# A Fourier mixer feeding a mixture of experts: expert rounds sized by the mean number of full blocks, from the first batch on, with the end of the last round under a condition

## The chip, the core and the metric

The kernel runs on one core of a Trainium2 chip. The core's engines work side by side, each through its own list of instructions: TensorE (PE, with PEld for its weight loads), VectorE (DVE), ScalarE (ACT), GpSimd (POOL) and SyncE (SP), which here only issues transfers. The metric is the device time of one execution in microseconds (us). Three executions of the kernel before took 744.09, 748.9 and 751.19 us, median 748.9.

## The reference

Two layers follow one another. The first filters each of 8 batches (2,496 rows of 256 numbers) along the rows in the frequency domain. The second sends each of the 19,968 filtered rows to one of 8 experts, the one with the highest score, and multiplies what the expert gives by the softmax weight of that score.

```python
X = np.fft.rfft(x, axis=1)
F = (filt_r + 1j * filt_i)[None, :, :]
y = np.fft.irfft(X * F, n=x.shape[1], axis=1)

logits = x @ w_gate + modality_bias[modality_id]
e_idx = np.argmax(logits, axis=1)
for e in range(E):
    mask = e_idx == e
    h = np.maximum(x[mask] @ w1[e], 0.0)
    out[mask] = gate_w[mask, None] * (h @ w2[e])
```

w1 is 256x1024 and w2 1024x256 for each expert. The inputs are drawn with a fixed seed. Counted in the reference, the experts get these rows after each batch (cumulative; experts 1, 2, 4, 5, 6 and 7 get none):

| after batch | 0 | 1 | 2 | 3 | 4 | 5 | 6 | 7 |
|---|---|---|---|---|---|---|---|---|
| expert 0 | 1258 | 2477 | 3744 | 4989 | 6227 | 7520 | 8767 | 9972 |
| expert 3 | 1238 | 2515 | 3744 | 4995 | 6253 | 7456 | 8705 | 9996 |

The kernel is not told this; its code is the same for any routing.

## The kernel before

**The transform.** A batch goes through three stages of small matrix products (`stage1`, `stage2`, `stage3`), each for a piece of the batch at a time. Between the stages the data go to DRAM and come back in another order: `b1_d` between the first two (stored at L238, loaded by `load_t2`, L433), `b2_d` between the last two (stored at L473, loaded by `load_t4`, L440). Both loads put their tiles into one pool, `bp` (L112), with three buffers under one tag. All of these stores and loads are issued by SP, in order.

**Routing.** `stage3` also computes the scores. `count` and `place` find each row's expert and its place, and `scatter` (L581, an indirect transfer issued by POOL) writes the row into that expert's bin in DRAM, `bins_d`. A batch has 20 scatters.

**Blocks and rounds.** Experts work on blocks of 256 rows of one bin. After a batch is placed, `table` (L599) computes, on DVE, which expert and which block each of the K next turns takes. K is a number that is fixed when the program is built, since the list of instructions is: the round sizes `KR` (L81). Before, a round is as long as the number of blocks that are full whatever the routing (`sure`): 0, 11, 10, 10, 9, 10, 10 after batches 0 to 6. The last round has 25 turns, enough for any routing (85 in all). A turn for which there is no block reads a bin of padding, whose rows are dropped at the output (`bounds_check` at L718).

**One turn.** `load` reads the number of the block and issues the load of its rows (`xs`, L659, on SP). `turn` copies the expert's w1 (L675, DVE) and transposes the rows (L685). Four steps follow, in each of which `up` (L696) makes a quarter of the hidden layer, ACT applies the relu (L701), and `down` (L709) takes a quarter of the turn before. After a turn's last step DVE multiplies by the weight (L716), and POOL scatters the 2x128 rows to `out` (L719).

**The order of work.** The main loop (L823) counts slots, `n`. In a slot stand one piece of each stage of each batch that is due, batches being 14 slots apart, up to a few scatters, and 2.25 expert steps (`STEPS`), if a turn is ready. A turn is not begun before 4 slots after its load (`LAG`). The weights w1 and w2 are loaded in slots 13 to 48. Batch g is placed in slot 45+14g, and its round is opened when its scatters are issued, 10 slots later. Up to slot 60 (`FRONT`, `alone`) the transform also uses PSUM tiles of the experts' pools (`front`, L219). The loop ends at slot 151, and the turns that are left follow alone (L861), the tail. A scheduler may move an instruction of one engine past others within what its dependences allow; it keeps the shape of this order.

Of the kernel before, what the change touches and what calls it, by code (L numbers as in the profile page):

```python
# [13 lines left out]
I32 = mybir.dt.int32  # L14
# [9 lines left out]
def cdiv(a, b):  # L24
    return (a + b - 1) // b
# [3 lines left out]
def kernel(  # L29
# [12 lines left out]
    nc = tc.nc  # L42

    B, S, D = x.shape
    NF = S // 2 + 1
    N = B * S
    E = moe_w_gate.shape[1]
# [22 lines left out]
    BLK = 256  # L70
# [4 lines left out]
    NBLK = cdiv(N, BLK) + E - 1  # L75
    DW = D // 2
    RW = DW + 2


    sure = [max(0, ((g + 1) * S - E * (BLK - 1)) // BLK) for g in range(B)]  # L80
    KR = [0, sure[1]] + [sure[g] - sure[g - 1] for g in range(2, B - 1)]  # L81
    KR.append(NBLK - sum(KR))

    b1_d = nc.dram_tensor("b1_d", (B, NTT, KA, D), BF16, kind="Internal").ap()
    b2_d = nc.dram_tensor("b2_d", (B, NS, KB, D), BF16, kind="Internal").ap()
# [2 lines left out]
    const_pool = ctx.enter_context(tc.tile_pool(name="const", bufs=1))  # L88
# [20 lines left out]
    SCH = 8  # L109
    xp = ctx.enter_context(tc.tile_pool(name="fx", bufs=3))  # L110
    rp = ctx.enter_context(tc.tile_pool(name="fr", bufs=2))
    bp = ctx.enter_context(tc.tile_pool(name="fbig", bufs=3))  # L112
    yp = ctx.enter_context(tc.tile_pool(name="fy", bufs=2))


    marks = {"ld": [], "up": [], "w1": [], "out": [], "pe": []}
# [64 lines left out]
    def ts(out, in_, s1, s2, op0=ALU.mult, op1=ALU.add):  # L181
        nc.vector.tensor_scalar(out, in_, scalar1=s1, scalar2=s2, op0=op0, op1=op1)
# [58 lines left out]
    def input_piece(g, k):  # L241

        stage1(g, k)
        if (k + 1) * EV in [t1 for t0, t1 in TCH]:
            load_x()
# [124 lines left out]
    ts(ecap, eio, float(CAP), -1.0)  # L370
    KMAX = max(KR)
    jio_i = const_pool.tile([P, KMAX], I32)
# [57 lines left out]
    def load_t2(g, c):  # L430
        src = b1_d[g].rearrange("t (jr s) c -> (t jr) s c", jr=4)
        t2 = bp.tile([KB, SCH, D], BF16, tag="t24", name="t2")
        nc.sync.dma_start(t2, src[:, c * SCH:(c + 1) * SCH, :])  # L433
        st[g]["t2", c] = t2
# [142 lines left out]
    def scatter(g, t):  # L577

        rows = P if t < NYF else KA
        with behind("out", 1):  # L580
            ins = nc.gpsimd.indirect_dma_start(  # L581
                out=bins_d[:, :], out_offset=IOA(ap=st[g]["pos"][:rows, t:t + 1], axis=0),
                in_=st[g]["yw"][:rows, t, :], in_offset=None)

        free_of(ins, "bins")
        free_of(ins, "bin_reads")
        tc.add_to_no_dep_group("bins", ins.ins)
        paced(ins)
# [10 lines left out]
    def table(K, last):  # L599

        b2 = [P, K, E]
        ni = tp_.tile([P, E], I32, tag="ni")
        av = tp_.tile([P, E], F32, tag="av")
        if last:
            ts(av, cnt, 1.0, float(BLK - 1))
            nc.vector.tensor_copy(ni, av)
        else:
            nc.vector.tensor_copy(ni, cnt)
        nc.vector.tensor_single_scalar(ni, ni, int(math.log2(BLK)), op=ALU.arith_shift_right)
        nc.vector.tensor_copy(av, ni)  # L610
        nc.vector.tensor_sub(av, av, done)
        incl = tp_.tile([P, E], F32, tag="incl")
        nc.vector.tensor_tensor_scan(incl, ones_sq[:, 0:E], av, 0.0, op0=ALU.mult, op1=ALU.add)
        excl = tp_.tile([P, E], F32, tag="excl")
        nc.vector.tensor_sub(excl, incl, av)
        v = tp_.tile([P, E], F32, tag="v")
        nc.vector.tensor_sub(v, done, excl)
        m = tp_.tile(b2, F32, tag="m")
        jb = jio[:, 0:K, None].to_broadcast(b2)
        nc.vector.tensor_tensor(m, incl[:, None, :].to_broadcast(b2), jb, op=ALU.is_le)  # L620
        ej = tp_.tile([P, K], F32, tag="ej")
        nc.vector.reduce_sum(ej, m, axis=AX.X)
        ec = tp_.tile([P, K], F32, tag="ec")
        nc.vector.tensor_scalar_min(ec, ej, float(E - 1))
        ej_i = tp_.tile([P, K], I32, tag="eji", bufs=3)
        nc.vector.tensor_copy(ej_i, ec)
        nc.vector.tensor_tensor(m, eio[:, None, :].to_broadcast(b2), ej[:, :, None].to_broadcast(b2),
                                op=ALU.is_equal)
        tmp = tp_.tile(b2, F32, tag="mt")
        nc.vector.tensor_mul(tmp, m, v[:, None, :].to_broadcast(b2))  # L630
        lb = tp_.tile([P, K], F32, tag="lb")
        nc.vector.reduce_sum(lb, tmp, axis=AX.X)
        nc.vector.tensor_add(lb, lb, jio[:, 0:K])
        bj = tp_.tile([P, K], F32, tag="bj")
        nc.vector.scalar_tensor_tensor(bj, in0=ej, scalar=float(BPE), in1=lb, op0=ALU.mult, op1=ALU.add)
        nc.vector.tensor_scalar_min(bj, bj, float(E * BPE))
        bj_i = tp_.tile([P, K], I32, tag="bji", bufs=3)
        nc.vector.tensor_copy(bj_i, bj)
        if not last:
            ts(excl, excl, -1.0, float(K))  # L640
            nc.vector.tensor_scalar_max(excl, excl, 0.0)
            nc.vector.tensor_tensor(excl, excl, av, op=ALU.min)
            nc.vector.tensor_add(done, done, excl)
        return ej_i, bj_i

    binv = bins_d.rearrange("(n p i) d -> n p i d", p=P, i=NI)

    def behind(what, n):

        m = marks[what]  # L650
        return tc.issue_after(m[-n]) if len(m) >= n else nullcontext()

    def load(tab, j, last):

        ej_i, bj_i = tab
        with behind("ld", 2):
            bj = nc.values_load(bj_i[0:1, j:j + 1], engines=(ET.SP,), min_val=0, max_val=E * BPE)
        xs = ep.tile([P, NI, RW], I32, tag="xs", bufs=5)
        ld = nc.sync.dma_start(xs, binv[ds(bj, 1)].rearrange("o p i d -> p (o i) d"))  # L659
        tc.add_to_no_dep_group("bin_reads", ld.ins)  # L660
        marks["ld"].append(ld.ins)
        return dict(xs=xs, ej_i=ej_i[0:1, j:j + 1], last=last)
# [63 lines left out]
    def pad_bins():  # L726

        end = tp_.tile([P, E], F32, tag="end")
        nc.vector.tensor_add(end, cnt, ecap)
        end_i = tp_.tile([P, E], I32, tag="endi")  # L730
        ts(end_i, end, 1.0, 1.0)
        for e in range(E):
            r = nc.values_load(end_i[0:1, e:e + 1], engines=(ET.SP,), min_val=0, max_val=E * CAP - BLK)
            ins = nc.sync.dma_start(bins_d[ds(r, BLK)].rearrange("(p i) w -> p i w", i=NI), pad)
            free_of(ins, "bins")
            free_of(ins, "bin_reads")
            tc.add_to_no_dep_group("bins", ins.ins)
# [57 lines left out]
    moe = Experts()  # L795
    tabs = {}
# [4 lines left out]
    def pace(left):  # L801

        if to_bins and left:
            g, t = to_bins[0]
            if t < NY:
                scatter(g, t)
                to_bins[0][1] += 1
                left -= 1
            else:
                if g == B - 1:  # L810
                    pad_bins()
                moe.open(tabs[g], KR[g], g == B - 1)
                to_bins.pop(0)
        return left

# [7 lines left out]
    while True:  # L823
        for g in range(1, B):
            if 0 <= n - g * GAP < NP:
                input_piece(g, n - g * GAP)
        for g in range(B):
            k = n - g * GAP - OFF2
            if (k + LEAD) % 4 == 0 and 0 <= k + LEAD < NS // EV:
                load_t2(g, (k + LEAD) // 4)  # L830
            if 0 <= k <= NS // EV:
                stage2(g, k)
        for g in range(B):
            k = n - g * GAP - OFF3
            if (k + LEAD) % 3 == 0 and 0 <= k + LEAD < NPY:
                load_t4(g, (k + LEAD) // 3)
            if 0 <= k <= NPY + 1:
                stage3(g, k)
            if k == NPY + 2:
                count(g)  # L840
            if k == NPY + 3:
                place(g)
                tabs[g] = table(KR[g], g == B - 1) if KR[g] else None
                to_bins.append([g, 0])
        alone[0] = n < FRONT
        left = 2 if n < (B - 1) * GAP + OFF3 + NPY + 3 else NY
        left = pace(pace(left) if n < FRONT + 10 else left)
        if n >= WSTART and n % 3:
            load_w()
        owed += STEPS  # L850
        while owed >= 1:
            owed -= 1
            outs = len(marks["out"])
            moe.step()
            if len(marks["out"]) == outs:
                left = pace(left)
        n += 1
        if not to_bins and n > (B - 1) * GAP + OFF3 + NPY + 4:
            break
    LAG = 0  # L860
    while moe.step():  # L861
        pass


# [28 lines left out]
```

## Time and profile before

| | us |
|---|---|
| median of three executions | 748.9 |
| the profiled execution | 804.45 |
| its span, from the first to the last instruction | 802.7 |
| TensorE busy | 633.6 |
| VectorE, ScalarE, GpSimd busy | 382.7, 387.6, 376.5 |
| mean granted TensorE clock | 0.842 of full |
| first and last w1 copy of a turn (L675) | 205.9, 785.4 |

Busy times are of engines that work side by side, so their sum says nothing; what matters in each stretch is which engine or transfer the others wait for. A granted clock of 0.50 says that the multiplying array ran at half speed. A wait on SP holds back every transfer queued behind it.

### The profile page before, as it was taken

Reading aid. Unit: us, or ns where it says so; the run is one execution under the profiler, and the core shown is the slowest. Engines: PE = TensorE matmul, PEld = TensorE weight load, DVE = VectorE, ACT = ScalarE, POOL = GpSimd, SP = SyncE. Lnnn points to the kernel's source line nnn. Section 1 sums busy time; section 2 is a strip of 40 time slices with the busy share of each in tenths; the row PEclk is TensorE's granted clock in tenths of the full one; section 3 lists DMA queues with packets and bytes.
Section 4 is the critical chain, followed back from the end, with each engine's and each line's share of the span. In section 5 each row is a group of like instructions: output and inputs, shape, how many; then the busy total and the mean of one; then the engine's idle time right before and its main releaser. Section 6 shows DMA issues by size and latency. Waiting matters only on the chain.

```text
span 802.7 us, 16037 instructions
## 1 busy us (share of the span) xinstructions
PE 633.6 (79%) x4886; PEld 491.6 (61%) x4886; DVE 382.7 (48%) x1226; ACT 387.6 (48%) x695; POOL 376.5 (47%) x421
## 2 busy tenths in 40 slices
PE   1454695997998987888778788978735999999995
PEld 0344573664666775677556567746624878877785
DVE  5432244445455555448444755634622444444442
ACT  1444554543456554566446445423412455555553
POOL 5032121644435645563644456466375444444444
PEclk9996557555559998999899899979966899999998
DMA  8799999975586575675444343422232333323310
GB/s 151 161 195 218 222 204 202 216 173 150 134 183 166 138 180 136 147 163 163 132 119 137 110 137 91 147 79 67 78 112 75 97 100 101 100 90 93 98 56 2
DMA packets 92825, 106.81 MB, mean 133 GB/s; under 512 B 12836, under 2 KB 75882, under 8 KB 92588
## 3 DMA queue, kind: packets, MB, share of 16 engines
q0 software_dynamic: 29248, 50.76, 27.4%
q1 hardware_dynamic: 63496, 55.03, 25.9%
q8 instruction: 44, 0.72, 0.4%
q14 instruction: 37, 0.30, 0.1%
HBM read 71.87 MB, written 54.31 MB: 157 GB/s over the span
## 4 chain that ended last, share of the span: by engine, by line
PE 44%; issue 21%; DMA 13%; POOL 7%; DVE 6%; ACT 4%; another core or an unknown queue 2%; SPq 1%; POOLq 0%; DVEq 0%; ACTq 0%
PE hps L696 9%; PE ops L709 8%; POOL out_dram L719 7%; DMA b_d<-t 4%; PE ps L497 3%; PE lt L509 3%; PE ps L496 3%; PE pz L458 3%; PE pz L457 3%; PE ps L449 3%; DMA out_dram<-osb,meta 2%; DMA b_d<-z 2%; ACT t L235 2%; DMA t<-b_d 2%
## 5 line engine op out<-in xcount | busy, mean ns | idle before, releaser
L701 ACT ACTIVATE hT<-hps 128x512 f16<-128x512 f32 x340 | 197.4, 598 | 236.0 <-PE hps L696 125.8
L719 POOL DMA_INDIRECT out_dram<-osb,meta x170 | 168.5, 991 | 180.5 <-DVE osb L716 129.2
L696 PE MATMUL hps<-xT,w 128*128 128x256 f16 x1360 | 222.2, 286 | 31.6 <-issue 25.2
L709 PE MATMUL ops<-w2sb,hT 128*128 x1360 | 221.6, 285 | 7.8 <-issue 7.3
L581 POOL DMA_INDIRECT bins_d<-yo,pos_i x160 | 161.2, 1007 | 115.9 <-issue 44.7
L709 PEld LDWEIGHTS <-hT 128*128 128x128 f16 x1360 | 138.8, 102 | 41.3 <-issue 16.6
L696 PEld LDWEIGHTS <-w 128*128 128x128 f16 x1360 | 129.7, 102 | 56.0 <-issue 31.9
L675 DVE COPY w<-w1sb 128x2048 f16 x85 | 59.9, 705 | 83.7 <-PE ops L709 45.1
L716 DVE TENSOR_SCALAR osb<-ops,meta 128x256 f32<-128x256 f32 x170 | 74.7, 477 | 16.6 <-PE hps L696 5.3
L471 ACT CAST z<-pz 104x512 f16<-104x512 f32 x96 | 56.8, 591 | 41.2 <-PE pz L458 16.1
L462 ACT CAST xf<-ps 104x512 f16<-104x512 f32 x96 | 56.2, 589 | 42.4 <-PE ps L449 27.8
L464 DVE TENSOR_TENSOR p<-xf,g 104x512 f16<-104x512 f16 x96 | 40.5, 422 | 67.6 <-ACT xf L462 56.5
L457 PE MATMUL pz<-p,a1m 104*104 104x256 f16 x192 | 63.0, 341 | 8.1 <-DVE p L464 6.2
L449 PE MATMUL ps<-t,w2m 104*104 104x256 f16 x192 | 47.9, 346 | 24.8 <-DMA t<-b_d 9.5
L686 DVE COPY xT<-pT 128x512 f16<-128x512 f16 x85 | 35.9, 423 | 60.7 <-PE pT L685 27.8
L458 PE MATMUL pz<-xf,a2m 104*104 104x256 f16 x192 | 62.6, 340 | 1.1 <-DVE xf L465 0.5
L518 DVE COPY yT<-lt 128x512 f16<-128x512 f16 x80 | 33.7, 422 | 61.1 <-PE lt L514 26.7
L231 PE MATMUL fp<-xt,w1m 96*96 96x256 f16 x114 | 33.1, 400 | 32.8 <-DVE w1m L206 17.0
L496 PE MATMUL ps<-t,wbm 96*96 96x256 f16 x118 | 37.9, 321 | 24.3 <-ACT t L235 13.7
L497 PEld LDWEIGHTS <-wbm 96*32 96x32 f16 x160 | 15.4, 96 | 61.1 <-issue 54.8
L231 PEld LDWEIGHTS <-w1m 96*96 96x96 f16 x208 | 31.0, 164 | 34.6 <-DVE w1m L206 17.0
L509 PE MATMUL lt<-ident,yo 128*128 128x128 f16 x320 | 38.5, 253 | 15.9 <-issue 9.6
(191 smaller groups left out, 700.4 us busy)
## 6 DMA issues: line engine op xcount, KB each, us to landing
xs<-bins_d SPq DMA_DIRECT2D x85, 130.0 KB
t<-b_d SPq DMA_DIRECT2D x24, 416.0 KB
b_d<-z SPq DMA_DIRECT2D x48, 208.0 KB
xt<-in_x_dram POOLq DMA_DIRECT2D x24, 384.0 KB
b_d<-t SPq DMA_DIRECT2D x48, 192.0 KB
t<-b_d SPq DMA_DIRECT2D x24, 384.0 KB
w1sb<-in_moe_w_dram POOLq DMA_DIRECT2D x16, 256.0 KB
w2sb<-in_moe_w_dram POOLq DMA_DIRECT2D x8, 512.0 KB
```

The costliest lines, as they stand in the source:

```text
L231: mm = nc.tensor.matmul(ps[:KA, i, :], lhsT=w1m, rhs=xt[:, t - t0 + i, :], start=True, stop=True)
L449: mm = nc.tensor.matmul(ps[:KB, i, :], lhsT=w2m[:, s + i, :], rhs=st[g]["t2", s // SCH][:, s % SCH + i, :], start=True, stop=True)
L457: nc.tensor.matmul(pz[:KB, i, :], lhsT=a1m[:, s_ + i, :], rhs=p1[:, i, :], start=True, stop=False)
L458: nc.tensor.matmul(pz[:KB, i, :], lhsT=a2m[:, s_ + i, :], rhs=p2[:, i, :], start=False, stop=True)
L496: nc.tensor.matmul(ps[:KA, i, :], lhsT=wbm, rhs=t4[:, t - t0, :], start=True, stop=True)
L509: nc.tensor.transpose(pT[:, i, dc, :], yo[:, ub + i, dc * P:(dc + 1) * P], ident)
L581: ins = nc.gpsimd.indirect_dma_start(out=bins_d[:, :], out_offset=IOA(ap=st[g]["pos"][:rows, t:t + 1], axis=0), in_=st[g]["yw"][:rows, t, ...
L696: mm = nc.tensor.matmul(hps[:, k, :], lhsT=b["w1"][:, dc, ft * P:(ft + 1) * P], rhs=b["xT"][:, dc].rearrange("p i t -> p (i t)"), start=(d ...
L701: nc.scalar.activation(b["hT"][:, q * FQ:(q + 1) * FQ, :], hps, AF.Relu)
L709: nc.tensor.matmul(b["ops"][:, i, :], lhsT=b["hT"][:, ft, i * P:(i + 1) * P], rhs=w2sb[:, ds(b["ej"], 1), ft, :], start=(ft == 0 and i == ...
L716: nc.vector.tensor_scalar_mul(osb[:, i, :], b["ops"][:, i, :], gate[:, i, :])
L719: ins = nc.gpsimd.indirect_dma_start(out=out[:, :], out_offset=IOA(ap=b["meta"][:, i, 0:1], axis=0), in_=osb[:, i, :], in_offset=None, **kw)
```

## The change

`KR` is computed from `hope`, the number of full blocks if each of the 8 bins ends in a half-filled block: 5, 15, 25, 35, 44, 54, 64 after batches 0 to 6, so rounds of 5, 10, 10, 10, 9, 10, 10. Batch 0 now has a table and a round. The last table has 25 entries as before, but of the last round only the first `FEW + 1` = 15 turns are opened unconditionally. Turns 15 to 18 and turns 19 to 24 stand in two conditional parts behind the tail, each run only if the number of blocks left, computed on the chip by the last table and read by all engines, is over 15 or over 19. The pool `bp` gets a fourth buffer.

```diff
     sure = [max(0, ((g + 1) * S - E * (BLK - 1)) // BLK) for g in range(B)]
-    KR = [0, sure[1]] + [sure[g] - sure[g - 1] for g in range(2, B - 1)]
-    KR.append(NBLK - sum(KR))
+    hope = [max(0, ((g + 1) * S - E * BLK // 2) // BLK) for g in range(B - 1)]
+    KR = [hope[0]] + [hope[g] - hope[g - 1] for g in range(1, B - 1)]
+    LEFT = NBLK - sure[B - 2]
+    FEW = cdiv(N, BLK) - hope[B - 2]
+    KR.append(LEFT)
+
+    PARTS = [0, FEW + 1, FEW + 5, LEFT]
...
-    bp = ctx.enter_context(tc.tile_pool(name="fbig", bufs=3))
+    bp = ctx.enter_context(tc.tile_pool(name="fbig", bufs=4))
...
-        if not last:
+        if last:
+            left_i = const_pool.tile([1, 1], I32, name="left_i")
+            nc.vector.tensor_copy(left_i, incl[0:1, E - 1:E])
+            return ej_i, bj_i, left_i
+        else:
...
-                moe.open(tabs[g], KR[g], g == B - 1)
+                moe.open(tabs[g], KR[g] if g < B - 1 else PARTS[1], g == B - 1)
...
-                tabs[g] = table(KR[g], g == B - 1) if KR[g] else None
+                tabs[g] = table(KR[g], g == B - 1)
...
     while moe.step():
         pass
+    left = nc.values_load(tabs[B - 1][2], min_val=0, max_val=LEFT)
+    for p0, p1 in zip(PARTS[1:], PARTS[2:]):
+        with tc.If(left > p0):
+            for m in marks.values():
+                m.clear()
+            moe = Experts()
+            moe.todo = [(tabs[B - 1], j, True) for j in range(p0, p1)]
+            while moe.step():
+                pass
```

More of the change, by code (lines that the diff above doesn't have):

```diff
@@ L80 @@
     sure = [max(0, ((g + 1) * S - E * (BLK - 1)) // BLK) for g in range(B)]
-    KR = [0, sure[1]] + [sure[g] - sure[g - 1] for g in range(2, B - 1)]
-    KR.append(NBLK - sum(KR))
+    hope = [max(0, ((g + 1) * S - E * BLK // 2) // BLK) for g in range(B - 1)]
+    KR = [hope[0]] + [hope[g] - hope[g - 1] for g in range(1, B - 1)]
+    assert all(hope[h] - hope[g] + sure[g] >= sure[h] for h in range(B - 1) for g in range(h))
+    LEFT = NBLK - sure[B - 2]
+    FEW = cdiv(N, BLK) - hope[B - 2]
+    KR.append(LEFT)
+    PARTS = [0, FEW + 1, FEW + 5, LEFT]
     b1_d = nc.dram_tensor("b1_d", (B, NTT, KA, D), BF16, kind="Internal").ap()
@@ L643, in table @@
             nc.vector.tensor_add(done, done, excl)
-        return ej_i, bj_i
+            return ej_i, bj_i
     binv = bins_d.rearrange("(n p i) d -> n p i d", p=P, i=NI)
@@ L653, in load @@
     def load(tab, j, last):
-        ej_i, bj_i = tab
+        ej_i, bj_i = tab[:2]
         with behind("ld", 2):
```

## The prediction

> **What bounds the kernel now.** I first read the page's 40 slices, which show a change of regime, and then summed each engine over the stretches between the placings of batches 0 to 7 (the placing products of L557 stand at 140.1, 186.4, 235.9, 302.6, 374.0, 446.8, 511.7 and 575.7 us), and over the tail. Columns: stretch, its length, busy us and instructions of PE, PEld, DVE, ACT, POOL, then granted clock, share of the transfer engines, GB/s.
>
> ```profile
> PEclk9996557555559998999899899979966899999998
> ...
> 140.10:186.40 46.30, 41.17 (x215) 28.12 (x215) 21.79 (x70) 23.47 (x43) 23.28 (x26) 0.50 0.80 188
> 186.40:235.90 49.50, 43.35 (x224) 29.27 (x224) 25.30 (x94) 23.28 (x42) 22.90 (x25) 0.50 0.64 148
> 235.90:302.60 66.70, 58.37 (x486) 46.09 (x486) 38.24 (x130) 39.40 (x74) 35.09 (x37) 0.91 0.66 171
> 302.60:374.00 71.40, 59.38 (x510) 46.38 (x510) 38.54 (x132) 41.02 (x76) 38.83 (x40) 0.93 0.59 149
> 374.00:446.80 72.80, 58.84 (x498) 45.52 (x497) 39.32 (x131) 38.96 (x72) 38.09 (x39) 0.93 0.48 136
> ...
> 618.80:789.70 170.90, 162.74 (x1442) 135.61 (x1442) 80.15 (x199) 92.17 (x161) 78.54 (x81) 0.97 0.28 87
> ```
>
> Between placings 0 and 2 there is no expert work: PE is busy 88% of the time at half clock, so PE sets the pace of 14 slots, about 48 us. From the third stretch on 14 slots carry 31.5 expert steps, 7.9 turns, the clock is over 0.9, and the stretch is 67 to 73 us. From 618.8 on only turns run, and PE is busy 95%. The groups of that tail (second number of a pair: mean ns; after the bar's second half: idle time before them):
>
> ```profile
> L709 PE MATMUL ops<-w2sb,hT 128*128 x640 | 101.4, 275 | 7.1 <-issue 6.7
> L696 PE MATMUL hps<-xT,w 128*128 128x256 f16 x642 | 98.2, 276 | 7.1 <-issue 6.1 <-ACT hT L701 1.0
> L701 ACT ACTIVATE hT<-hps 128x512 f16<-128x512 f32 x161 | 92.6, 597 | 78.7 <-PE hps L696 51.9 <-PE ops L709 24.5 <-PE pT L685 1.5
> ```
>
> ACT waits for PE, PE for almost nothing: the tail is bound by PE. Its timeline shows fours of these products every 0.435 us, and the w1 copies follow one another from 631.0 to 785.4 us in 37 equal steps, so a turn in the tail costs 154.4 / 37 = 4.17 us. In the mixed part SP's waits matter (from 235 to 580 us: total, times, longest):
>
> ```profile
> SPq L659 <- DMA bins_d<-yo,pos_i: 93.9, 29, 7.0
> ...
> SPq L440 <- PE ps L449: 8.3, 4, 3.9
> ...
> SPq L433 <- PE hps L696: 5.0, 1, 5.0
> SPq L433 <- PE ps L497: 3.1, 2, 2.6
> ```
>
> The first: a turn's load of rows waits for scatters that stand before it, and the transform's loads and stores wait behind it. The others: a transform load waits until a product has freed its buffer.
>
> **Turns removed and turns moved.** Only two experts get rows, 9972 and 9996, so there are 39 + 40 = 79 blocks. The kernel before makes 85 turns, 6 of them on padding. After the change the rounds of batches 0 to 6 take 64 blocks (walking the counts through `table`, each round finds enough full blocks: the first has 8 to choose 5 from), and 15 are left: exactly the 15 unconditional turns. 19,968 rows are 78 blocks exactly, so two experts can never need more than 79, whatever way close scores fall, and both conditions are false. Walking the loop for both kernels: before, turns begin at slot 73, and 45 have begun when the loop ends at slot 151; 169 steps are left. After, batch 0's round opens at slot 55, its five turns begin at slot 59 and are done by 69, and from 73 on both kernels run alike, without a gap; 50 turns have begun and 125 steps are left. So the tail loses 44 steps, 11 turns: 6 were padding, 5 have moved to slots 59 to 69. **The tail gains 11 x 4.17 = 45.9 us.** Its products run at full clock without waits, so this sum should hold outside the profile too.
>
> **What the five turns cost where they go.** They go into the stretch from 186.4 to 235.9 us, where no row shows expert work. Nearest are the three stretches after it: (66.7 + 71.4 + 72.8 - 3 x 49.5) / 23.6 turns = 62.4 / 23.6 = 2.64 us a turn, 13.2 for five; that already holds their loads on SP, their w1 copies on DVE, relus on ACT and ten output scatters on POOL (about 1 us each, POOL being busy 46% here). It is less than in the tail because the clock goes up with them. Upper bound: the clock stays at half, and all PE work adds up: a turn has 32 products of 256 columns (0.213 us at half clock, twice 0.435 / 4 of the tail) and 4 transposes (0.107), 7.2 us, five are 36. Lower bound: at full clock the transform's 43 us of PE work shrink to 22 and five turns add 18, 40 together, less than the 49.5 there now; other chains then bind, and the cost could be 0 or some us less. [...] The row says 0.50 for 96 us, and 0.92 in the ten us from 240, when the first turn runs. [...] **+13**, with 0 and 36 as ends.
>
> **The fourth buffer.** The waits for a buffer's release in the mixed part are 8.3 + 5.0 + 3.1 and smaller ones, about 20 us of SP's time. Of PE's stalls over 0.8 us, those before a product that reads a loaded tile first (L449, L496) sum to 26, but most of the loads concerned stood behind an L659 wait, which stays. The schedule after puts some of the transform's loads ahead of a turn's loads. Bounds: 20 us gained; lost, if the loads now wait in SP's queue for their own stores to land (see the rivals). I take **-4**.
>
> **Table 0 and the end.** Some 25 small DVE instructions come with batch 0's table, at about the 0.16 us of L527's additions, 4 us on an engine that is half idle; those that delay a transform product cost perhaps **+1** (0 to 4). At the end every engine reads `left` and jumps over two parts. Reading a register from SBUF takes 0.7 to 0.9 us on SP's timeline. PE, which has the longest jumps, is done 5 us before POOL; on POOL the read and the jumps lie beside the landing of the last output (3.4 to 3.8 us in the chain), and the end waits for that landing anyway, but in the kernel before the last turns write nothing and the span ends 3 us after the last scatter. [...] I take **+2**, for the landing that now comes last (0 to 7).
>
> **The sum.** -45.9 + 13 - 4 + 1 + 2 = -34 us. The profiled execution would go from 804.45 (span 802.7 and 1.75 around it) to about 770. It is 7% longer than the median of 748.9, but the tail's rate can't be what is longer, so I take the 34 us off the median unscaled: **715 us**, 4.5% faster.
>
> **Rivals.** (1) The clock stays at half in slots 59 to 69: 36 for 13, so -11: 738 us. For it: five turns last only ten slots, some 40 us, with the transform between. Against: the clock rose within 5 us of the first turn at 243. (2) The lower bound holds: turns almost free (2), buffers worth 10: -51, 698. (3) Slower: the fourth buffer moves transform loads ahead in SP's in-order queue, and what was a wait for a free buffer becomes a wait for the load's own store to land, with the other stores and the turns' rows behind it. Before, such waits are 22.8 us in 8 (L433) and 11.7 in 6 (L440). There are 56 of these loads; from 0.7 us each on the path, 38 us without the buffer's gain, it decides. At 1 us each: 748.9 - 38 + 56 = 767. Against: the store is on the load's path in any case. (4) The change doesn't do what it says: a third expert gets a row on the chip, 16 blocks are left and the first part runs: four turns and a refill of the pipeline, 4 x 4.17 + 10 = 27, so 742.
>
> **Numbers.** The forecast has 0.70 (own range 703 to 727, the spread of the turns' and buffers' costs), rival 1 0.10, rival 2 0.13, rival 3 0.05, rival 4 0.02. The three timed runs lie 0.9% apart, so 1% is about what can be told from no change. Faster by over 1%: 0.92; within: 0.03; slower: 0.05. The range takes in half of rival 2, and rival 1: 699 to 738.
>
> **What would show it.** Right: the first expert products near 190 us instead of 243; a clock over 0.8 between 195 and 230; the stretch between placings 1 and 2 about 62 us; a tail of 31 turns at 4.17; 158 outputs (L719 before), no record from the conditional parts. Wrong: a clock of 0.5 in that stretch, more SP waits for landing stores, records from the parts, or a tail turn over 4.3 us.

## The result, and the profile after

On the chip where it was first timed the changed kernel takes 719.8 us (median of four, 718.3 to 722.8) against 750.1 for the kernel before (four, 744.1 to 752.9): ratio 0.961, 95% interval 0.954 to 0.968. The experiments ran on other chips, on which both kernels are slower and the gain is smaller: on one 793.5 against 807.1 us (0.985, 0.975 to 0.994), on another 806.5 against 818.5 us (0.987, 0.983 to 0.991). I call the first chip A, and the chips of the experiments B, C and D, in the order in which they come below. What sets A apart, the chip or its state at the time, is not known. The profile shown before the prediction took 804.45 us, as the kernel does on B and C, not on A.

The profile after is from A: span 718.1 us, device time 720.3. The clock row of its page, then the stretches between its placings (141.3, 188.4, 240.9, 305.7, 371.1 and 430.5 us) and the steady tail, with the columns of the windows shown before:

```profile
PEclk9999555575699689999999999999999799999995
```

```profile
141.30:188.40 47.10, 37.89 (x230) 26.35 (x231) 25.63 (x99) 24.08 (x46) 24.18 (x27) 0.64 0.85 202
188.40:240.90 52.50, 47.28 (x397) 36.44 (x396) 32.81 (x113) 33.63 (x62) 33.39 (x35) 0.89 0.66 165
240.90:305.70 64.80, 59.18 (x488) 46.82 (x487) 37.20 (x132) 40.30 (x74) 35.10 (x37) 0.88 0.69 176
305.70:371.10 65.40, 57.11 (x510) 45.12 (x510) 38.15 (x132) 41.74 (x76) 39.09 (x42) 0.97 0.65 170
...
588.40:690.00 101.60, 101.60 (x981) 91.02 (x979) 55.17 (x132) 65.06 (x109) 52.32 (x55) 1.00 0.33 103
```

The second stretch now holds the five moved turns, at clock 0.89 where it was 0.50. The first expert product is at 186.9 us, just ahead of it. Windows of 5 and 30 us around the start of the five turns:

```profile
185.00:190.00 5.00, 3.68 (x22) 3.08 (x23) 3.29 (x17) 1.44 (x3) 0.00 (x0) 0.50 0.69 177
190.00:195.00 5.00, 5.00 (x24) 3.37 (x23) 3.45 (x19) 2.65 (x6) 2.23 (x3) 0.52 0.62 158
195.00:200.00 5.00, 4.94 (x46) 4.02 (x45) 2.82 (x16) 4.10 (x8) 4.08 (x4) 1.00 0.61 152
200.00:230.00 30.00, 29.78 (x273) 23.09 (x271) 18.93 (x51) 21.02 (x39) 21.98 (x24) 1.00 0.67 164
230.00:260.00 30.00, 23.12 (x153) 17.31 (x153) 16.90 (x74) 14.73 (x28) 12.03 (x14) 0.72 0.66 177
```

The clock is full some 8 us after the first turn begins, and falls back in the pause after the fifth (no expert product from 231.4 to 243.4 us): it is 1.00 from 231 to 235 us, 0.57 from 235 to 240 and 0.50 from 240 to 243. In the tail PE no longer waits at all:

```profile
L721 PE MATMUL ops<-w2sb,hT 128*128 x437 | 66.3, 273 | 0.0
L708 PE MATMUL hps<-xT,w 128*128 128x256 f16 x436 | 65.4, 273 | 0.0
L713 ACT ACTIVATE hT<-hps 128x512 f16<-128x512 f32 x109 | 65.1, 597 | 36.7 <-PE hps L708 36.7
```

and the w1 copies follow one another every 3.74 us, where the first profile of before had 4.17. SP's waits in the mixed part (241 to 545 us; a q marks an engine's sequencer, which waits, branches and issues) are of the same kind as before:

```profile
SPq L671 <- DMA bins_d<-yo,pos_i: 146.6, 39, 14.1
...
SPq L448 <- DMA b_d<-z: 8.8, 4, 2.9
SPq L441 <- DMA b_d<-t: 5.9, 2, 4.8
SPq L441 <- PE ps L457: 4.9, 3, 2.9
```

The first has grown from 93.9 us, but between placings 2 and 7 it is 81 to 123 us on B, C and D, in the kernel before and in the changed one alike. There are 158 output scatters, and no record from the conditional parts' bodies. What is new is at the end. The records at the line of the conditions (PE's and POOL's), and the closing drain, POOL's longest instruction, at the last line (operation, engine, count, then min/median/max in ns, first and last start):

```profile
L877 PEldq COMPARE_BRANCH  x2: 3658/4168/4677, 694.8 to 698.8; - x2
L877 POOLq COMPARE_BRANCH  x2: 45/48/50, 696.7 to 705.4; - x2
L877 POOLq INC_SWDGE_SEM  x2: 2297/2312/2327, 703.0 to 706.1; - x2
```

```profile
L909 POOLq DRAIN  x3: 51/109/8805, 708.5 to 717.8; - x3
```

The last output scatter is over at 698.8 us, and the span ends at 718.1: 19 us in which no engine computes. The prediction had 2 us more for this end than before.

### The profile page after: what moved, and what is told of

The parts are those of the page before. It is cut to its first block, busy times and chain, and to the rows that moved or that the text cites. A ratio compares the mean times of both kernels' runs of the same rounds, so it can differ in the third digit from the quotient of the medians.

```text
span 718.1 us, 15390 instructions
## 1 busy us (share of the span) xinstructions
PE 571.4 (80%) x4670; PEld 453.9 (63%) x4670; DVE 367.4 (51%) x1219; ACT 379.6 (53%) x671; POOL 364.2 (51%) x409
## 5 line engine op out<-in xcount | busy, mean ns | idle before, releaser
L713 ACT ACTIVATE hT<-hps 128x512 f16<-128x512 f32 x316 | 188.4, 597 | 174.1 <-PE hps L708 172.4
L708 PE MATMUL hps<-xT,w 128*128 128x256 f16 x1264 | 204.7, 283 | 36.9 <-DVE xT L698 36.3
L731 POOL DMA_INDIRECT out_dram<-osb,meta x158 | 156.5, 990 | 126.6 <-DVE osb L728 76.0
L721 PE MATMUL ops<-w2sb,hT 128*128 x1264 | 196.8, 279 | 0.3 <-issue 0.3
L708 PEld LDWEIGHTS <-w 128*128 128x128 f16 x1264 | 117.1, 101 | 58.9 <-DVE xT L698 38.8
L721 PEld LDWEIGHTS <-hT 128*128 128x128 f16 x1264 | 126.1, 100 | 19.3 <-issue 0.7
L693 DVE COPY meta<-xs 128x4 int32<-128x4 int32 x79 | 14.4, 183 | 116.2 <-DMA xs<-bins_d 107.3
L728 DVE TENSOR_SCALAR osb<-ops,meta 128x256 f32<-128x256 f32 x158 | 69.3, 476 | 4.9 <-PE ops L721 4.8
L457 PEld LDWEIGHTS <-w2m 104*104 104x104 f16 x192 | 26.2, 153 | 35.0 <-issue 24.8
L134 POOL DMA_DIRECT2D xt<-in_x_dram x32 | 19.6, 614 | 48.4 <-PE fp L239 45.7
```

The costliest lines, as they stand in the source:

```text
L457: mm = nc.tensor.matmul(ps[:KB, i, :], lhsT=w2m[:, s + i, :], rhs=st[g]["t2", s // SCH][:, s % SCH + i, :], start=True, stop=True)
L708: mm = nc.tensor.matmul(hps[:, k, :], lhsT=b["w1"][:, dc, ft * P:(ft + 1) * P], rhs=b["xT"][:, dc].rearrange("p i t -> p (i t)"), start=(d ...
L713: nc.scalar.activation(b["hT"][:, q * FQ:(q + 1) * FQ, :], hps, AF.Relu)
L721: nc.tensor.matmul(b["ops"][:, i, :], lhsT=b["hT"][:, ft, i * P:(i + 1) * P], rhs=w2sb[:, ds(b["ej"], 1), ft, :], start=(ft == 0 and i == ...
L728: nc.vector.tensor_scalar_mul(osb[:, i, :], b["ops"][:, i, :], gate[:, i, :])
L731: ins = nc.gpsimd.indirect_dma_start(out=out[:, :], out_offset=IOA(ap=b["meta"][:, i, 0:1], axis=0), in_=osb[:, i, :], in_offset=None, **kw)
```

## Experiments

**Four programs on chip B**, where the kernel before takes 808.4 us.

The kernel before, unchanged:

> The kernel before, unchanged, on the chip of the other runs of this set. Two readings of its first profile (804.5 us, a tail turn of 4.17 us, where the changed kernel's profile has 720.3 us and 3.74 us) are to be told apart. Theory A: the first profile is of an execution that was slower throughout, and the kernel before has tail turns of about 3.75 us and a profiled time of 745 to 755 us. Theory B: 4.17 us belongs to the order of its instructions, and its tail turns take 4.1 to 4.2 us again, 0.4 us more than after the change, which then alone is worth 42 x 0.43 = 18 us. Against the kernel before, a ratio of 1.00 under both.

Measured: 807.1 us, ratio 0.999 (0.996 to 1.002), profiled 802.2, a tail turn 4.17 us. So the first profile was not of an odd execution: it is what this kernel does on a chip like B. Theory A as worded is refuted, and B not shown, since the changed kernel was not in this set; but `after_buf3`, below, is nearly the changed kernel, and also has 4.17 us here.

The padding turns left out, and nothing else:

```diff
-    KR.append(NBLK - sum(KR))
+    KR.append(cdiv(N, BLK) + 1 - sum(KR))
```

> The kernel before with a last round of 19 turns instead of 25: the six turns on padding are left out, and nothing else changes (right for this routing alone). The prediction's theory: six tail turns less, at 4.17 us 25.0 us, at the changed kernel's 3.74 us 22.4 us: 725 to 728 us, ratio 0.967 to 0.970. Rival (the gain is that of the turns moved into the mixed part): padding turns are cheaper than others, since their rows are dropped, and the ratio is above 0.98.

Measured: 790.3 us, ratio 0.980 (0.974 to 0.985), 18 us less, at the rival's bound. Padding turns are not cheaper: all tail turns take 4.17 us, and six are 25. The missing part is at the end: from the last w1 copy to the end of the span it is 23.1 us (757.8 to 780.9) where before_again has 17.3 (783.2 to 800.5). The closing drain:

```profile
L888 POOLq DRAIN  x3: 51/113/11750, 768.3 to 780.6; - x3
```

It returns at 780.1 us, 8.8 us after the last scatter is over (771.3). With padding turns at the end it returns 1.6 us after it. So the 6 turns covered 5.8 us of ending, and their removal is worth 19 by this account, not 25 (18 measured).

The fourth buffer, taken from the changed kernel and given to the kernel before:

```diff
-    bp = ctx.enter_context(tc.tile_pool(name="fbig", bufs=4))
+    bp = ctx.enter_context(tc.tile_pool(name="fbig", bufs=3))
```

> The changed kernel with three buffers for the transform's loads, as before, instead of four. The prediction's theory: the fourth buffer is worth 4 us, so 724 us, ratio to the kernel before 0.966. Rival 2: it is worth 10 us or more: 730 us, 0.973. Rival 3: it costs, and this is faster than 720 us.

```diff
-    bp = ctx.enter_context(tc.tile_pool(name="fbig", bufs=3))
+    bp = ctx.enter_context(tc.tile_pool(name="fbig", bufs=4))
```

> The kernel before with the fourth buffer alone. The prediction's theory: -4 us, 746 us, ratio 0.995. Rival 2: -10 us or more, 0.987 or less. Rival 3: slower than the kernel before by 1% or more.

Measured: after_buf3 791.9 us, 0.978 (0.969 to 0.986); before_buf4 804.9 us, 0.997 (0.993 to 1.001). The second is the clean one: 3.4 us less, which fits the 4 of the prediction and can't be told from nothing. Neither 10 us nor a loss is there, so rivals 2 and 3 fall as to the buffer in the kernel before. after_buf3 says little, as the changed kernel was not on this chip; what the buffer is worth in the changed kernel is not shown.

**Four programs on chip C**, where the kernel before takes 807.1 us.

The two kernels, unchanged:

> The kernel before once more, for its profile beside that of the changed kernel on one chip. The first profile and the set before this one had 4.17 us for a tail turn in all four programs, the changed kernel's own profile 3.74 us, and the kernel before took 750 us where the change was timed and 808 us on the chip of the set. Theory A: the time of a tail turn belongs to the chip; the two kernels have the same tail turn here, 4.17 us with a kernel before near 805 us, or 3.74 us with one near 750 us. Theory B: it belongs to the program; then it is 4.17 us here and 3.74 us in after_again.

> The changed kernel, unchanged. Theory A (the chip): the same tail turn as the kernel before on this chip. The prediction's sum: 34 us less than the kernel before, ratio 0.955 to 0.962. From after_buf3 (0.978) and before_buf4 (0.997) on the chip of the set before: 0.975, if the buffer is worth the same 3 us here, and then the five moved turns cost more than the 13 us of the prediction: the stretch between placings 1 and 2 is 62 to 65 us.

Measured: 807.9 us (1.001, 0.997 to 1.006) and 793.5 us (0.985, 0.975 to 0.994); a tail turn is 4.18 us in the one and 4.16 in the other. The program that had 3.74 us on A has 4.16 here: the change doesn't decide the time of a turn, as theory A has it (that the chip does is not shown). The account below uses these two profiles. The stretch with the five turns (for before_3, the columns as above, then for after_again):

```profile
187.70:237.10 49.40, 43.39 (x225) 29.30 (x225) 25.37 (x95) 23.25 (x42) 22.84 (x25) 0.50 0.65 153
```

```profile
187.30:247.70 60.40, 49.34 (x396) 36.67 (x396) 32.99 (x112) 34.13 (x63) 33.47 (x35) 0.90 0.61 148
```

It is 11.0 us longer. And the ends, the scatters last (start, duration; idle time before it):

```profile
805.13 0.98 POOL L719 DMA_INDIRECT out_dram<-osb,meta  x1 [0.30 <-issue]
806.41 0.98 POOL L719 DMA_INDIRECT out_dram<-osb,meta  x1 [0.30 <-issue]
```

```profile
L888 POOLq DRAIN  x3: 51/261/5391, 803.6 to 810.0; - x3
```

```profile
769.36 0.98 POOL L731 DMA_INDIRECT out_dram<-osb,meta  x1 [0.30 <-DVEq L877]
770.65 0.98 POOL L731 DMA_INDIRECT out_dram<-osb,meta  x1 [0.30 <-issue]
```

```profile
L877 PEldq COMPARE_BRANCH  x2: 4103/4260/4417, 767.6 to 772.0; - x2
L877 POOLq COMPARE_BRANCH  x2: 45/48/50, 769.3 to 777.9; - x2
L877 POOLq INC_SWDGE_SEM  x2: 2297/2312/2327, 775.6 to 778.7; - x2
```

```profile
L909 POOLq DRAIN  x3: 51/109/8805, 781.1 to 790.4; - x3
```

Before, the longest drain begins at 803.6 us, while POOL is still at its last scatters, and returns at 809.0, 1.6 us after they are over (807.4). After, POOL is through with its scatters at 771.6. It waits until the outputs have landed (the last signal of it comes at 775.3), spends from 775.6 on 2.3 us on an increment of an output semaphore for the first skipped part, about 0.8 on the second branch and waits that are long met, 2.3 on the second increment, and then drains for 8.8. TensorE's two jumps take 4.1 and 4.4 us, but are over at 776.8.

The conditions taken away, and then six padding turns put back as well:

```diff
-    left = nc.values_load(tabs[B - 1][2], min_val=0, max_val=LEFT)
-    for p0, p1 in zip(PARTS[1:], PARTS[2:]):
...
```

> The changed kernel without the two conditional parts and the reading of the number of blocks left: the tail ends after the 15 turns (right for this routing alone). The prediction's theory: 2 us less than the changed kernel at most, since only the end of the chain differs. [...]

```diff
-                moe.open(tabs[g], KR[g] if g < B - 1 else PARTS[1], g == B - 1)
+                moe.open(tabs[g], KR[g] if g < B - 1 else PARTS[1] + 6, g == B - 1)
```

> after_noif with a last round of 21 turns, six of them on padding as in the kernel before: only the five turns are moved, nothing is left out. The prediction's theory: six tail turns more than after_noif, 22 to 25 us; against the kernel before -5 turns in the tail (19 to 21 us), +13 for them in the mixed part, -4 for the buffer: 10 to 12 us faster, ratio 0.986. If the moved turns cost as much in the mixed part as in the tail, the ratio is 0.995 to 1.00.

Measured: after_noif 782.2 us, 0.973 (0.963 to 0.983), 11 us less than the changed kernel, where 2 at most were expected. Its end, from the last w1 copy on, is 23.0 us (754.1 to 777.1), that of after_again 32.5 (758.2 to 790.7): 9.5 of the 11 us are there. The drain:

```profile
L900 POOLq DRAIN  x3: 51/113/11725, 764.5 to 776.8; - x3
```

returns at 776.3, again 8.8 us after the last scatter (767.5). after_pad6 800.6 us, 0.991 (0.986 to 0.995): the six padding turns are worth 18.4 us (800.6 - 782.2), not 22 to 25, as in before_last19. With all 85 turns, moving five and the buffer are worth 6.5 us, against 10 to 12 expected and 0 to 4 under the alternative. Five turns less in the tail save 20.9 us, so by the medians all else became some 14 us longer. The stretch of the moved turns shows 11.3 of it in this profile (60.7 against 49.4 us), 2.3 us a turn.

**One condition in place of two.** The account says that each skipped part costs in series.

```diff
-    PARTS = [0, FEW + 1, FEW + 5, LEFT]
+    PARTS = [0, FEW + 1, LEFT]
```

> The changed kernel with one conditional part (turns 15 to 24) in the place of two. Theory (each skipped part costs in series at the end, on POOL: a wait for the landed outputs, then an increment of the output semaphores of 2.3 us, and the closing drain returns 8.8 us after the last such increment): from the first increment to the second 3.15 us fall away, the drain still returns 8.8 us after the one that is left, and the time from the last output scatter to the end goes from 19.1 to about 16 us. Rival 1 (the landing of the outputs is what the end waits for): the end is unchanged within 1 us. Rival 2 (TensorE's two branches of 4.1 to 4.4 us each set the end): 4.5 us or more fall away.

> The kernel before for its profile, on another chip if one comes. If the tail turn belongs to the chip, a chip on which it takes about 750 us shows 3.74 us here, and one on which it takes about 808 us shows 4.17 us. If it is 4.17 us at about 750 us, the program decides.

Measured on chip D: after_oneif 796.7 us against 818.9, 0.973 (0.966 to 0.981). From the last scatter to the end it is 13.4 us (780.4 to 793.8) where after_again had 19.1. The drain still takes 8.80 us and follows the one increment. Of the 5.7 us, 3.15 are the second part's, and the rest is that the increment, which waits for the landing, came 1.4 us after the last scatter and not 3.9. Rival 2's number (4.5 us or more) would fit the 5.7 as well; the order in the traces speaks against it. TensorE is past its jump at 780.9, and POOL's increment starts at 781.8, 0.3 us after the last signal of a landed output (781.5), as in after_again (775.3 and 775.6). before_4: 819.6 us, 0.998 (0.994 to 1.002), a tail turn 4.23 us; a kernel before near 750 us was not met again.

> One conditional part again, beside the changed kernel with its two on the same chip. The end after the last output scatter was 19.1 us with two parts and 13.4 us with one on two different chips, of which the landing of the outputs (3.9 and 1.4 us before the first increment) is 2.5 us and may be chance. Theory: one skipped part is worth 3.15 us of POOL's time, so 3 to 6 us less than after_3, 0.4 to 0.8% of the time.

> The changed kernel, third chip of these sets. If the kernel before takes about 808 us here and a tail turn 4.17 us, the ratio is 0.975 to 0.985, as in after_again; if it takes about 750 us and a tail turn 3.74 us, it is 0.96, as in the first timing.

Measured side by side, on D again: one condition 798.2 us (793.7 to 802.5, six), 0.977 (0.973 to 0.982); two 806.5 us (803.2 to 810.9, six), 0.987 (0.983 to 0.991). The version with one condition is 8 us faster than the changed kernel and 20 us faster than the one before; it still takes any routing, but runs all ten turns of the part where one more is needed. Its ending:

```profile
L877 POOLq INC_SWDGE_SEM  x1: 2336/2336/2336, 783.7 to 783.7; - x1
```

```profile
L909 POOLq DRAIN  x3: 51/109/8805, 786.1 to 795.4; - x3
```

From the last w1 copy to the end are 28.8 us (766.9 to 795.7) here and 32.9 (768.8 to 801.7) in after_3, so the end explains 4 of the 8 us. In these two profiles placing 7 comes 1.8 us earlier (600.3 against 602.1). The rest isn't placed.

## Why the prediction was right, and where it was not

On A the kernel was 30 us faster, where 34 were forecast, and 719.8 us lie near the predicted 715 and inside the range. But the sum was made against a profile of a slower chip, and there it can be checked term by term, with before_3 and after_again. The w1 copies and the placings (two products each, 0.1 us apart; the table has the first) of the two:

```profile
L675 DVE COPY w<-w1sb x85: 681/694/923, 207.2 to 793.1; 128x2048 f16 x85
L557 PE MATMUL psO<-c,Lexcl x16: 218/277/361, 141.2 to 584.3; 128*128 128x8 f32 x16
```

```profile
L687 DVE COPY w<-w1sb x79: 678/694/859, 164.8 to 758.2; 128x2048 f16 x79
L565 PE MATMUL psO<-c,Lexcl x16: 218/277/363, 141.6 to 593.8; 128*128 128x8 f32 x16
```

| term | predicted, us | measured on C, us | from |
|---|---|---|---|
| 11 tail turns less | -45.9 | -44.4 | placing 7 to last w1 copy: 208.9 to 164.5 |
| five turns, buffer, table 0 (13 - 4 + 1) | +10 | +9.5 | placing 7: 584.2 to 593.7 |
| the end | +2 | +15.3 | last w1 copy to end of span: 17.2 to 32.5 |
| sum | -34 | -19.6 | span: 810.3 to 790.7 |

The sum of this pair is 5 us more than the medians on C differ by (807.9 - 793.5 = 14.4). The profiled execution of before_3 was the slowest of its eight (812.1 us), and its tail and end (226.0 us) are no longer than those of before_again (227.6), so its excess lies ahead of placing 7, in the second row. That row's agreement is thus partly luck: the medians of after_pad6 give some 14 us, and the profiles of before_4 and after_3 on D 15.7 (placing 7 at 586.4 and 602.1).

**Bound and turns.** Right: 79 turns, 15 left, both parts skipped, so rival 4 is out; the tail is bound by PE (busy 101.6 of 101.6 us from 588.4 on, on A).

**The moved turns.** In their own stretch right: 11.0 us for five on C and 12.7 on D, 13 predicted, and 60.4 and 61.8 us for the stretch, about 62 predicted (52.5 on A). The clock did what was forecast: 1.00 from 195 to 230 us on A, 0.90 over the stretch on C. Full clock came within 8 us of the first turn on A (in the profile of before, from 242 us on, 3.5 us after the first expert product, which stands at 238.5 and not at 243), so rival 1 is out, and rival 2's nearly free turns are out too. (Twice 0.435 / 4 is 0.218 and not 0.213, so rival 1's bound is 37 us and not 36; nothing rests on it.) But the whole of the mixed part, for which +10 stood, grew by 10 to 16 us; what makes up the difference isn't placed, and table 0 was not tried by itself.

**The buffer.** 3.4 us on B, where the interval reaches from 5.3 to a loss of 0.7: not refuted, not shown. Rival 3, the slower one, did not occur. Its sign hardly shows: between placings 2 and 7 SP waits for landing stores 12.5 us in after_again and 11.9 in after_3, where before_3 has 6.6 and before_4 11.7, far from the 38 us that it needs.

**The end.** This step failed: "on POOL the read and the jumps lie beside the landing of the last output (3.4 to 3.8 us in the chain), and the end waits for that landing anyway", with 0 to 7 us as its ends. It was taken from where the branches stand, not from what a skipped part must still do. Two things were missing. For each skipped part POOL makes an increment of an output semaphore, 2.3 us, after the landing; the profile of before could have no row of it. And the closing drain returns 8.8 us after the last scatter with rows, or after the last such increment. Its row in the profile of before showed only 5.4 us, over 1.6 us after the last scatter: padding turns stood between the last real output and the end, so by this reading it had all but run out by then (the endings of all these programs agree with that; it was not tried by itself). Without padding the end is 5.8 us longer (before_last19), and with two skipped parts 9.5 more (after_again against after_noif): 15.3. I did name that "in the kernel before the last turns write nothing", but priced it at 2 us.

**The jumps.** PE's two jumps take 3.7 and 4.7 us on A and 4.1 and 4.4 on C, POOL's, past 8 and 12 scatters, 0.05 us each. What PE's time there goes into is not shown. It is off the path: PE is done at 704.0 us on A, 14 us before the span ends, and at 776.8 on C, again 14 before it. No run shows the 7 us at the top of the range that was given for the end; what the runs show in its place is the 15.3 us above, on POOL.

**The profile and the median.** "The tail's rate can't be what is longer" was wrong: on A a tail turn of the changed kernel takes 3.74 us. If the kernel before has the same there, 11 are 41, not 46. With +10 to +16 for the mixed part and +15.3 for the end that would leave a gain of 10 to 16 us on A, where 30 were measured. So something worth some 14 to 20 us more was gained on A. No profile of the kernel before from A exists, and it can't be placed. The forecast was near the mark there with an end that is 13 us short and something unknown that made up for it, which is luck; on C and D, where the kernel gained 14 and 12 us, the same sum is over twice the gain. That it was inside the range should be read with that.

## What to carry to other kernels

Work that a condition skips was not free here, where it holds scatters that POOL issues (2.3 us of POOL for each skipped part, and an end 9.5 us longer with two of them): look at what the engine still does when a part is skipped, and try one condition in place of several. Sum the end of the span as a stretch of its own, from the last computing instruction on; useless work at the end may be hiding a drain (5.8 us of it here), and then only its removal beyond that is gain. A sum made from one profile should be compared with medians from the same chip before it is moved to another.

## What was not expected of the hardware

The same program takes 3.74 us for a tail turn on A and 4.16 to 4.24 on C and D, with products of the same length (mean 273 ns on A, 272 on C). The tail's groups in after_again show the difference as waits:

```profile
L721 PE MATMUL ops<-w2sb,hT 128*128 x451 | 70.2, 272 | 5.0 <-issue 4.7
L713 ACT ACTIVATE hT<-hps 128x512 f16<-128x512 f32 x112 | 64.3, 596 | 51.9 <-PE hps L708 33.7 <-PE ops L721 18.2
```

By the profile's releasers, one relu in nearly every turn (25 of 28) starts only after the group of products behind its own (ops, 18.2 us in all), which on A does not happen (all its waits are for hps). A turn is 0.43 us longer, about one group. Whether this late start is the cause, and why it is there, remains open. In the mixed part, too, the stretches on A are shorter, 53 to 65 us after placing 2 where C has 64 to 77.
